# Attention and two feed-forward layers on one core: the second layer's matmul operands placed in either 64-byte half of a 128-byte stretch

## Chip, core and metric

One Trainium2 chip, one of its cores. The metric is the device time of one execution of the whole program, in microseconds; of several executions the median is given.

## What is computed

Three stages follow each other, all in fp32 accuracy. A Performer attention (random features, exponentials, a quotient) on q, k and v gives 2304 tokens of 512 features; two feed-forward layers act on these:

```python
def _moe_ref(x, w_a, w_b, w_out) -> np.ndarray:      # d_model 512, d_ff 1536
    a = x @ w_a
    b = x @ w_b
    return (a * b @ w_out).astype(np.float32)
...
def _moe2_ref(x, w_in, w_out) -> np.ndarray:         # d_model 512, d_ff 2048
    h = np.maximum(x @ w_in, 0.0)
    return (h * h @ w_out).astype(np.float32)
...
    x = np.ascontiguousarray(attn_out.transpose(0, 2, 1, 3)).reshape(B * S, H * D)
    x = _moe_ref(x=x, **moe_kwargs)
    return _moe2_ref(x=x, **moe2_kwargs)
```

Inputs are drawn in double precision; a weight arrives as two 32-bit words an element.

## The kernel before

**Split operands.** TensorE works on `float32r`. To keep fp32 accuracy each operand is held as a high part and a low part, and each product is three matmuls: high·high, high·low, low·high. `TERMS` (pairs of stationary part, moving part) is `((0, 0), (0, 1), (1, 0))`, so of three matmuls that follow each other the moving part goes high, low, high and the stationary part high, high, low. ScalarE and VectorE make the parts: `split` (L145 to L175) for weights, L728 and L729 for the tokens of the second layer, L784 to L787 for the hidden values.

**Stages.** Attention runs up to about 535 us, from 150 us on beside the first layer (phase A, `a_units`, matmuls of L610 and L635). The second layer (phase B, `b_units`) runs from about 650 us to the end. It is the part that the change touches.

**Phase B.** The 2304 tokens are cut into five blocks (`BB`): four of 512 and one of 256. For each block the loop over f goes through 16 slices of 128 hidden features. A slice takes 12 matmuls of L777 (four chunks kc of 128 input features, three terms each): stationary is a 128x128 piece of the weight `wi2[f]`, moving is the token tile `ys[i]`, 512 columns wide, 256 in the last block. ScalarE takes the sum out of PSUM with a Relu (L784), VectorE squares it (L785), ScalarE writes the high part (L786) and VectorE the low part (L787) into the tile `ss`. Then `outs(f - 1)` issues the matmuls of L764 of the slice before: for each 128 tokens of the block three matmuls, 12 in a wide block and 6 in the last. There stationary is a piece of `ss`, moving is `wo2[f]`, 512 columns in all blocks. So the stream of TensorE is 12 of L777, 12 (or 6) of L764, and so on; the hidden values of a slice are wanted one slice later.

**Where the tiles lie.** A weight pair (`wi2[f]` and `wo2[f]`) is one tile of `get_pair`, laid out `[pair, part, 512]`. Slice 0 has a pool of its own (`w2`), slices 1 to 12 reuse the 12 buffers of phase A's weights (`w`), slices 13 to 15 have a third pool (`w2r`). The token tile is `[chunk, part, columns]`, `ss` is `[part, columns]`. As the program is built, every `float32r` operand of phases A and B, moving or stationary, starts at a multiple of 128 bytes in its partition. In the attention there is another case: the tile `S`, stationary in the matmuls of L351 (moving is `OM`, 256 columns, at a multiple of 128), starts at byte 139,968 on the k side, which is 64 past a multiple of 128, and at byte 153,056 on the q side, which is 96 past one. The 128-column pieces of `S` lie 512 bytes apart, so they all keep that place.

**What sets the order.** One stream of instructions for each engine, in the order of the code; tiles in pools bring the waits. TensorE's weight load is an instruction of its own that runs beside the matmul ahead of it (engine PEld in the rows).

Of the kernel before, what the change touches and what calls it, by code (L numbers as in the profile page):

```python
# [9 lines left out]
F32R = mybir.dt.float32r  # L10
I32 = mybir.dt.int32
U32 = mybir.dt.uint32
U16 = mybir.dt.uint16
ACTF = mybir.ActivationFunctionType
ALU = mybir.AluOpType
# [20 lines left out]
def f32(ap):  # L36
    return ap.bitcast(F32)
# [7 lines left out]
def kernel(  # L45
# [17 lines left out]
    FA = w_out.shape[0] // 128  # L63
    FB = w_out2.shape[0] // 128
    KC = DM // 128
    NP = H // 2
    SM = 512
    ST = S - SM
# [73 lines left out]
    def split(raw, t):  # L142

        n = raw.shape[1]
        up = raw[:, :, :, 1]
        u = raw[:, :, :, 0]
        a = top["cut"].tile([128, 2, 512], F32, tag="a", name="a")[:, 0:n]
        p = top["cut"].tile([128, 2, 512], F32, tag="p", name="p")[:, 0:n]  # L150
        nc.scalar.activation(out=a, in_=f32(up), func=ACTF.Copy, scale=WORD_SCALE)  # L151
        nc.scalar.activation(  # L152
            out=u, in_=raw.bitcast(U16)[:, :, :, 1], func=ACTF.Copy, scale=2.0 ** 7,
        )
        nc.vector.tensor_scalar(
            out=i32(p), in0=i32(a), scalar1=3, scalar2=0x7FFFF000,
            op0=ALU.logical_shift_left, op1=ALU.bitwise_and,
        )
        nc.vector.scalar_tensor_tensor(  # L159
            out=i32(p), in0=i32(a), scalar=-0x80000000, in1=i32(p),  # L160
            op0=ALU.bitwise_and, op1=ALU.bitwise_or,
        )
        nc.scalar.copy(out=t[:, :, 0, :], in_=p)
        nc.vector.scalar_tensor_tensor(  # L164
            out=u.bitcast(U32), in0=up.bitcast(U32), scalar=23, in1=u.bitcast(U32),
            op0=ALU.logical_shift_left, op1=ALU.bitwise_or,
        )
        nc.vector.tensor_scalar(
            out=i32(a), in0=i32(p), scalar1=-0x00800000, scalar2=None,
            op0=ALU.bitwise_and,  # L170
        )
        nc.vector.scalar_tensor_tensor(
            out=t[:, :, 1, :], in0=u.bitcast(U32), scalar=2.0 ** -43, in1=a,
            op0=ALU.mult, op1=ALU.mult,
        )  # L175

# [26 lines left out]
        while any(x[1] == key for x in waiting):  # L203
            split_next()

    def get_pair(key, steps, pool, tag, *parts):
        t = pool.tile([128, 2, 2, 512], F32R, tag=tag, name=tag)
        load_split(key, parts, t, steps)
        return t[:, 0], t[:, 1]


    actx = ExitStack()
# [386 lines left out]
    def a_units():  # L599
# [4 lines left out]
        g_t, yp, part = {}, {}, {}  # L604

        def proj(ps, w, x):
            wv = w.rearrange("p a (k f) -> p a k f", k=KC)
            for kc in range(KC):
                for s_, m_ in TERMS:
                    nc.tensor.matmul(  # L610
                        ps, lhsT=wv[:, s_, kc, :], rhs=x[..., kc, m_, :],
                        start=(kc == 0 and (s_, m_) == TERMS[0]),
                        stop=(kc == KC - 1 and (s_, m_) == TERMS[-1]),
                    )
# [99 lines left out]

    wi2, wo2 = {}, {}

    BB = [(i * N, min(2, NBLK - i) * N) for i in range(0, NBLK, 2)]
    ys = {}
    op_pool = []

    def y_load(i, pool):
        w_ = BB[i][1]
        t = pool.tile([128, KC, 2, w_], F32R, tag="yx", name=f"yx{i}")
        ys[i] = t
        for c in range(KC):
            r = ypool.tile([128, w_], F32, tag="ys", name="yraw")
            nc.sync.dma_start(out=r, in_=y_d[i][:, c, :])
            nc.scalar.copy(out=t[:, c, 0, :], in_=r)  # L728
            nc.vector.tensor_tensor(  # L729
                out=t[:, c, 1, :], in0=r, in1=f32(t[:, c, 0, :]), op=ALU.subtract  # L730
            )

    def out_rows(c0):

# [17 lines left out]
    def b_units(i):  # L752


        y = ys[i]
        c0, w_ = BB[i]
        s_t, op = {}, {}

        def outs(f):
            for t in range(w_ // 128):  # L760
                if f == 0:
                    op[t] = bank(t, [128, DM], f"o{t}")
                for s_, m_ in TERMS:
                    nc.tensor.matmul(  # L764
                        op[t], lhsT=s_t[f][:, s_, t * 128:(t + 1) * 128], rhs=wo2[f][:, m_, :],
                        start=(f == 0 and (s_, m_) == TERMS[0]),
                        stop=(f == FB - 1 and (s_, m_) == TERMS[-1]),
                    )

        gp = wide_pool[0]  # L770
        for f in range(FB):
            need(("b", f))
            ps = bank(4 + f % 4, [128, w_], "ph")
            wv = wi2[f].rearrange("p a (k f) -> p a k f", k=KC)
            for kc in range(KC):
                for s_, m_ in TERMS:
                    nc.tensor.matmul(  # L777
                        ps, lhsT=wv[:, s_, kc, :], rhs=y[:, kc, m_, :],
                        start=(kc == 0 and (s_, m_) == TERMS[0]),
                        stop=(kc == KC - 1 and (s_, m_) == TERMS[-1]),  # L780
                    )
            r = gp.tile([128, w_], F32, tag="t", name="r")
            s_t[f] = gp.tile([128, 2, w_], F32R, tag="gs", name="ss")
            nc.scalar.activation(out=r, in_=ps, func=ACTF.Relu, scale=1.0 / W_SCALE)  # L784
            nc.vector.tensor_tensor(out=r, in0=r, in1=r, op=ALU.mult)  # L785
            nc.scalar.copy(out=s_t[f][:, 0, :], in_=r)  # L786
            nc.vector.tensor_tensor(  # L787
                out=s_t[f][:, 1, :], in0=r, in1=f32(s_t[f][:, 0, :]), op=ALU.subtract
            )
            if f:  # L790
                outs(f - 1)
            yield f
        outs(FB - 1)
        for t in range(w_ // 128):
            o = op_pool[0].tile([128, DM], F32, tag="o", name="o_s")
            nc.scalar.mul(out=o, in_=op[t], mul=1.0 / W_SCALE)
            for p0, cnt, r0, st in out_rows(c0 + 128 * t):
                nc.sync.dma_start(
                    out=out[r0:r0 + st * (cnt - 1) + 1:st, :], in_=o[p0:p0 + cnt, :]
                )  # L800
# [36 lines left out]
    def get_wo(n):  # L837
        if n >= len(wo_order):
            return
        pi, f = wo_order[n]  # L840
        if f in wo_made:
            need(("o", f))
            wo[pi, f] = wop.tile([128, 2, 512], F32R, tag="wo", name="wo")
            nc.sync.dma_start(out=f32(wo[pi, f]), in_=wo_d[f])
        else:
            wo_made.add(f)
            wo[pi, f] = wop.tile([128, 2, 512], F32R, tag="wo", name="wo")
            load_split(
                ("o", f), [(w_out, f, True)], wo[pi, f].unsqueeze(1), 3,
                lambda: nc.sync.dma_start(out=wo_d[f], in_=f32(wo[pi, f])),  # L850
            )

# [5 lines left out]
    def get_w2():  # L858
# [7 lines left out]
            po = (wpool, "w")  # L866
        else:
            po = (w2["r"], "w2r")
        wi2[f], wo2[f] = get_pair(("b", f), 1, *po, (w_in2, f, False), (w_out2, f, True))

    W_FIRST = 2

# [122 lines left out]
```

## Time and profile before

| | |
|---|---|
| median of three runs | 1052.57 us (1050.89 to 1053.95) |
| the profiled execution | 1052.61 us |
| its span, first to last instruction | 1050.8 us |
| TensorE matmul busy | 1024.0 us, 97% of the span |
| weight loads busy (beside the matmuls) | 873.6 us, 83% |
| VectorE, ScalarE busy | 526.8 us (50%), 471.2 us (45%) |
| granted TensorE clock, mean | 0.998 of 2.4 GHz |

A matmul's shown duration runs from its start to the arrival of its last result; since matmuls are pipelined, the next one starts long before. What a matmul costs is the distance from start to start. It is read from the chain of the work that ended last, or from the timeline, which merge equal matmuls: the time of a group of 12 divided by 12. The duration still tells something: it grows when a matmul is held up on its way.

### The profile page before, as it was taken

The page shows a single profiled execution, that of the slowest core. Times are in us where ns is not written, and L with a number is a line of the kernel's source. Part 1 is how long each engine was busy: PE and PEld are TensorE (multiplying, and loading weights), DVE is VectorE, ACT ScalarE, POOL GpSimd, SP SyncE. Part 2 cuts the span into 40 slices and gives each one's busy share as a digit, 9 for nine tenths or more (in the row PEclk, how much of TensorE's full clock was granted, in tenths as well). Part 3 has the DMA queues.
Part 4 walks back from the last instruction along what each step waited for, and adds up shares of the span by engine and source line. Part 5 has one row for each costly group of instructions (what it writes and reads, how often), then busy time and mean ns, then how long its engine had stood idle before and what let it go on. Part 6 is the DMA issues. An engine that isn't in the chain of part 4 may idle for free.

```text
span 1050.8 us, 14948 instructions
## 1 busy us (share of the span) xinstructions
PE 1024.0 (97%) x5641; PEld 873.6 (83%) x5641; DVE 526.8 (50%) x1274; ACT 471.2 (45%) x1079; POOL 28.9 (3%) x54
## 2 busy tenths in 40 slices
PE   4899999999999999999999999999999999999998
PEld 3789989999988877788888888788788888888887
DVE  4788885665654445444337987722222322322222
ACT  4887757554455443333326665522322322322232
POOL 3100101000000000000000000000000000000000
PEclk9999999999999999999999999999999999999999
DMA  6846864663432211312227664300200200100010
GB/s 166 242 148 205 267 233 120 210 209 95 142 105 80 63 46 56 95 62 70 66 87 264 230 220 174 107 1 0 81 1 1 71 1 1 51 1 1 0 41 21
DMA packets 83144, 105.90 MB, mean 101 GB/s; under 512 B 26240, under 2 KB 65152, under 8 KB 83072
## 3 DMA queue, kind: packets, MB, share of 16 engines
q1 hardware_dynamic: 81536, 103.37, 30.7%
q0 software_dynamic: 1536, 1.58, 0.5%
q8 instruction: 45, 0.74, 0.3%
q14 instruction: 27, 0.22, 0.1%
HBM read 87.62 MB, written 17.30 MB: 100 GB/s over the span
## 4 chain that ended last, share of the span: by engine, by line
PE 88%; DVE 4%; DMA 3%; ACT 3%; issue 1%; SPq 1%; ACTq 0%; DVEq 0%
PE abw L610 19%; PE o L764 19%; PE ph L777 18%; PE y L635 12%; PE ab L610 7%; PE ps_n L481 3%; PE ps_p L285 2%; PE ps_kv L423 2%; PE ps_p L351 2%; PE ps_qt L474 1%; DMA raw<-in_moe_w_out_dram 1%; PE ps_t L330 1%; DMA qn<-in_q_dram 1%; DVE p L159 1%; PE ps_x L492 1%
## 5 line engine op out<-in xcount | busy, mean ns | idle before, releaser
L635 PE MATMUL y<-gs,wo 128*128 128x256 f32 (+1 forms) x864 | 177.2, 345 | 0.0
L764 PE MATMUL o<-w,ss 128*128 128x512 f32 x702 | 170.9, 390 | 1.4 <-ACT ss L786 1.4
L777 PE MATMUL ph<-yx,w 128*128 128x512 f32 (+1 forms) x780 | 169.8, 368 | 0.0
L777 PEld LDWEIGHTS ph<-yx,w 128*128 128x128 f32 x780 | 137.4, 188 | 25.3
L785 DVE TENSOR_TENSOR r<-r 128x512 f32<-128x512 f32 (+1 forms) x80 | 51.1, 639 | 209.8 <-ACT r L784 209.8
L764 PEld LDWEIGHTS o<-w,ss 128*128 128x128 f32 x702 | 130.5, 188 | 29.7 <-ACT ss L786 2.2
L635 PEld LDWEIGHTS y<-gs,wo 128*128 128x128 f32 x864 | 136.6, 190 | 15.2
L610 PE MATMUL abw<-x_all,w 128*128 128x512 f32 x576 | 146.6, 398 | 0.0
L784 ACT ACTIVATE r<-ph 128x512 f32<-128x512 f32 (+1 forms) x80 | 44.5, 556 | 208.4 <-PE ph L777 208.2
L610 PE MATMUL ab<-x_all,w 128*128 128x256 f32 x864 | 132.9, 295 | 0.3 <-DVE x_all L549 0.2
L610 PEld LDWEIGHTS abw<-x_all,w 128*128 128x128 f32 x576 | 105.5, 189 | 19.2
L610 PEld LDWEIGHTS ab<-x_all,w 128*128 128x128 f32 x864 | 115.0, 193 | 1.5 <-DVE x_all L549 0.5
L787 DVE TENSOR_TENSOR ss<-r,ss 128x512 fp32r<-128x512 f32 (+1 forms) x80 | 51.1, 639 | 46.6 <-ACT ss L786 40.0
L610 PE MATMUL abw<-x_mid,w 128*128 128x512 f32 x288 | 73.1, 400 | 0.0
L786 ACT CAST ss<-r 128x512 fp32r<-128x512 f32 (+1 forms) x80 | 46.2, 577 | 51.5 <-DVE r L785 51.5
L610 PEld LDWEIGHTS abw<-x_mid,w 128*128 128x128 f32 x288 | 52.1, 189 | 9.8
L358 DVE CUSTOM_DVE_ANT_0 c<-ps_p,c 128x128 f32<-128x128 f32 x152 | 37.8, 287 | 32.5 <-ACT c L356 32.0
L701 ACT CAST gs<-a_s 128x256 fp32r<-128x256 f32 (+1 forms) x96 | 40.6, 433 | 28.3 <-DVE a_s L700 28.1
L164 DVE SCALAR_TENSOR_TENSOR raw<-raw 128x1024 uint32<-128x1024 uint32 (+1 forms) x40 | 42.5, 1062 | 13.4 <-ACT raw L152 13.3
L152 ACT ACTIVATE raw<-raw 128x1024 int32<-128x1024 uint16 (+1 forms) x40 | 40.8, 1020 | 11.4 <-DMA raw<-in_moe_w_out_dram 9.3
L702 DVE TENSOR_TENSOR gs<-a_s,gs 128x256 fp32r<-128x256 f32 (+1 forms) x96 | 42.8, 454 | 5.3 <-ACT gs L701 4.2
L151 ACT ACTIVATE a<-raw 128x1024 f32<-128x1024 f32 (+1 forms) x40 | 40.6, 1014 | 10.9 <-DMA raw<-in_moe_w_out_dram 5.6
(109 smaller groups left out, 1212.9 us busy)
## 6 DMA issues: line engine op xcount, KB each, us to landing
wo<-wo_d SPq DMA_DIRECT2D x60, 512.0 KB, 3.5
raw<-in_moe_w_out_dram SPq DMA_DIRECT2D x28, 512.0 KB, 4.8
raw<-in_moe_w_in_dram SPq DMA_DIRECT2D x16, 512.0 KB, 3.9
raw<-in_moe_w_a_dram SPq DMA_DIRECT2D x12, 512.0 KB, 4.8
raw<-in_moe_w_b_dram SPq DMA_DIRECT2D x12, 512.0 KB, 6.1
wo_d<-wo SPq DMA_DIRECT2D x12, 512.0 KB, 3.4
kn<-in_k_dram SPq DMA_DIRECT2D x16, 256.0 KB, 3.5
V<-in_v_dram SPq DMA_DIRECT2D x16, 256.0 KB, 3.4
```

Of the source, the lines that this page charges most:

```text
L151: nc.scalar.activation(out=a, in_=f32(up), func=ACTF.Copy, scale=WORD_SCALE)
L152: nc.scalar.activation(out=u, in_=raw.bitcast(U16)[:, :, :, 1], func=ACTF.Copy, scale=2.0 ** 7,)
L164: nc.vector.scalar_tensor_tensor(out=u.bitcast(U32), in0=up.bitcast(U32), scalar=23, in1=u.bitcast(U32), op0=ALU.logical_shift_left, op1=A ...
L610: nc.tensor.matmul(ps, lhsT=wv[:, s_, kc, :], rhs=x[..., kc, m_, :], start=(kc == 0 and (s_, m_) == TERMS[0]), stop=(kc == KC - 1 and (s_, ...
L635: nc.tensor.matmul(y_part(pi, f, c), lhsT=wo[pi, f][:, s_, c * 128:(c + 1) * 128], rhs=g[:, m_, :],  start=(f == f0 and (wide or c % 2 == ...
L702: nc.vector.tensor_tensor(out=g[:, 1, c], in0=a_s, in1=f32(g[:, 0, c]), op=ALU.subtract)
L764: nc.tensor.matmul(op[t], lhsT=s_t[f][:, s_, t * 128:(t + 1) * 128], rhs=wo2[f][:, m_, :], start=(f == 0 and (s_, m_) == TERMS[0]), stop=( ...
L777: nc.tensor.matmul(ps, lhsT=wv[:, s_, kc, :], rhs=y[:, kc, m_, :], start=(kc == 0 and (s_, m_) == TERMS[0]), stop=(kc == KC - 1 and (s_, m ...
L784: nc.scalar.activation(out=r, in_=ps, func=ACTF.Relu, scale=1.0 / W_SCALE)
L785: nc.vector.tensor_tensor(out=r, in0=r, in1=r, op=ALU.mult)
L786: nc.scalar.copy(out=s_t[f][:, 0, :], in_=r)
L787: nc.vector.tensor_tensor(out=s_t[f][:, 1, :], in0=r, in1=f32(s_t[f][:, 0, :]), op=ALU.subtract)
```

## The change

Only the places of phase B's operands change; the number, the kind, the order and the waits of all instructions are as before on every engine, row for row.

- `get_pair` makes the tile of a weight pair 1024 words for each of its two halves as before, or, with `odd` given, 1056 words. A word is four bytes, and `LINE` is 16 words, 64 bytes. With `odd=(a, b)` the high part starts `64*a` bytes after a multiple of 128, the low part `64*b` bytes. This is used for the slices 13 (1, 1), 14 (0, 1) and 15 (1, 0). It holds for both weights of a pair, the stationary one of L777 and the moving one of L764.
- `y_load` puts 64-byte gaps between the eight pieces of a token tile so that the piece of chunk c and part m starts at `64 * (Y_ODD[i % 4](c, m) mod 2)` past a multiple of 128: c + m in blocks 0 and 4, m in block 1, c in block 2, 0 in block 3.
- `ss` gets a gap too: `S_ODD` gives the places of its high and low part, (0, 0) in blocks 0 and 4, (0, 1) in block 1, (1, 1) in block 2, (1, 0) in block 3.
- `split` and `load_split` get the two parts as two views. Of phase A's operands none moves. The token tiles grow by 512 bytes a partition, `ss` by 128, the three last weight buffers by 256; the pools around them move by multiples of 128 bytes.

Below, a place is called odd when it is 64 bytes past a multiple of 128, else even. Counted over the built program of the changed kernel, in phase B:

| block | columns of L777 | L777 matmuls followed by a matmul whose moving operand has the other place | the same for L764 | place of `ss`, high and low |
|---|---|---|---|---|
| 0 | 512 | 190 of 192 | 20 of 192 | even, even |
| 1 | 512 | 129 of 192 | 19 of 192 | even, odd |
| 2 | 512 | 63 of 192 | 19 of 192 | odd, odd |
| 3 | 512 | 1 of 192 | 19 of 192 | odd, even |
| 4 | 256 | 191 of 192 | 10 of 95 | even, even |

So 470 matmuls with 512 columns and 191 with 256 are followed by a moving operand of the other place. The stationary operand that is loaded beside a matmul has the other place than this matmul's moving operand for 659 matmuls with 512 columns and 98 with 256. Before, all these counts are zero.

```diff
+    LINE = 16
+    SPAN = 1024 + 2 * LINE
...
-        nc.scalar.copy(out=t[:, :, 0, :], in_=p)
+        nc.scalar.copy(out=t[0], in_=p)
...
-            out=t[:, :, 1, :], in0=u.bitcast(U32), scalar=2.0 ** -43, in1=a,
+            out=t[1], in0=u.bitcast(U32), scalar=2.0 ** -43, in1=a,
...
-    def get_pair(key, steps, pool, tag, *parts):
-        t = pool.tile([128, 2, 2, 512], F32R, tag=tag, name=tag)
-        load_split(key, parts, t, steps)
-        return t[:, 0], t[:, 1]
+    def get_pair(key, steps, pool, tag, *parts, odd=None):
+        t = pool.tile([128, 2, SPAN if odd else 1024], F32R, tag=tag, name=tag)
+        at = (LINE * odd[0], 512 + LINE * (2 - odd[1])) if odd else (0, 512)
+        hi, lo = (t[:, :, o:o + 512] for o in at)
+        load_split(key, parts, (hi, lo), steps)
+        return [(hi[:, x], lo[:, x]) for x in range(2)]
...
+    Y_ODD = [lambda c, m: c + m, lambda c, m: m, lambda c, m: c, lambda c, m: 0]
+    S_ODD = [(0, 0), (0, 1), (1, 1), (1, 0)]
+    W_ODD = {13: (1, 1), 14: (0, 1), 15: (1, 0)}
...
-        t = pool.tile([128, KC, 2, w_], F32R, tag="yx", name=f"yx{i}")
-        ys[i] = t
+        t = pool.tile([128, KC * 2 * w_ + 2 * KC * LINE], F32R, tag="yx", name=f"yx{i}")
+        ys[i] = {}
+        for c in range(KC):
+            for m in range(2):
+                o = (2 * c + m) * (w_ + LINE) + LINE * ((2 * c + m + Y_ODD[i % 4](c, m)) % 2)
+                ys[i][c, m] = t[:, o:o + w_]
...
-                        op[t], lhsT=s_t[f][:, s_, t * 128:(t + 1) * 128], rhs=wo2[f][:, m_, :],
+                        op[t], lhsT=s_t[f][s_][:, t * 128:(t + 1) * 128], rhs=wo2[f][m_],
...
-                        ps, lhsT=wv[:, s_, kc, :], rhs=y[:, kc, m_, :],
+                        ps, lhsT=wi2[f][s_][:, kc * 128:kc * 128 + 128], rhs=y[kc, m_],
...
-            s_t[f] = gp.tile([128, 2, w_], F32R, tag="gs", name="ss")
+            st = gp.tile([128, SPAN], F32R, tag="gs", name="ss")
+            s_t[f] = tuple(
+                st[:, o:o + w_]
+                for o in (LINE * S_ODD[i % 4][0], 512 + LINE * (2 - S_ODD[i % 4][1]))
+            )
...
-        wi2[f], wo2[f] = get_pair(("b", f), 1, *po, (w_in2, f, False), (w_out2, f, True))
+        wi2[f], wo2[f] = get_pair(("b", f), 1, *po, (w_in2, f, False), (w_out2, f, True), odd=W_ODD.get(f))
```

## Rows read from the trace of the kernel before

**Rows 1.** The page: engines, the granted clock, the chain by engine and line.

```profile
PE 1024.0 (97%) x5641; PEld 873.6 (83%) x5641; DVE 526.8 (50%) x1274; ACT 471.2 (45%) x1079; POOL 28.9 (3%) x54
...
PEclk9999999999999999999999999999999999999999
...
PE 88%; DVE 4%; DMA 3%; ACT 3%; issue 1%; SPq 1%; ACTq 0%; DVEq 0%
PE abw L610 19%; PE o L764 19%; PE ph L777 18%; PE y L635 12%; PE ab L610 7%; PE ps_n L481 3%; PE ps_p L285 2%; PE ps_kv L423 2%; PE ps_p L351 2%; PE ps_qt L474 1%; DMA raw<-in_moe_w_out_dram 1%; PE ps_t L330 1%; DMA qn<-in_q_dram 1%; DVE p L159 1%; PE ps_x L492 1%
```

**Rows 2.** Busy time by stretch of phase B, in us, with counts and granted clock.

```profile
661.00:750.00 89.00, 88.52 (x389) 72.44 (x388) 34.43 (x49) 29.63 (x48) 0.00 (x0) 1.00 0.13 42
750.00:825.00 75.00, 75.00 (x332) 61.91 (x331) 20.53 (x30) 17.98 (x30) 0.00 (x0) 1.00 0.00 1
835.00:910.00 75.00, 75.00 (x333) 62.10 (x332) 18.65 (x28) 16.76 (x29) 0.00 (x0) 1.00 0.00 0
914.00:998.00 84.00, 84.00 (x372) 69.54 (x372) 21.93 (x32) 20.97 (x35) 0.00 (x0) 1.00 0.03 13
```

**Rows 3.** Chain in order of time: start, us, engine and line; a wide block.

```profile
805.20 2.72 PE o L764 x12
```

**Rows 4.** Timeline of TensorE, wide block: start, us, instructions; moving operand from both pools.

```profile
802.32 2.88 PE L777 MATMUL ph<-yx,w 128*128 128x512 f32 x12
805.04 2.88 PE L764 MATMUL o<-w,ss 128*128 128x512 f32 x12
807.76 2.88 PE L777 MATMUL ph<-yx,w2r 128*128 128x512 f32 x12
810.48 2.88 PE L764 MATMUL o<-w,ss 128*128 128x512 f32 x12
```

**Rows 5.** Timeline of TensorE in the last block.

```profile
1007.24 1.55 PE L764 MATMUL o<-w,ss 128*128 128x512 f32 x6
1008.63 1.60 PE L777 MATMUL ph<-yx,w 128*128 128x256 f32 x12
1010.06 1.55 PE L764 MATMUL o<-w,ss 128*128 128x512 f32 x6
```

**Rows 6.** Durations in ns, min/median/max: line 764 in 750 to 820 us.

```profile
L764 PE MATMUL o<-w,ss x144: 389/389/389, 750.6 to 813.0; 128*128 128x512 f32 x144
```

**Rows 7.** The same, lines 764 and 777 in the last block, 1007 to 1043 us.

```profile
L764 PE MATMUL o<-w,ss x72: 389/394/398, 1007.2 to 1039.4; 128*128 128x512 f32 x72
...
L777 PE MATMUL ph<-yx,w x124: 277/283/283, 1006.8 to 1035.3; 128*128 128x256 f32 x124
```

**Rows 8.** One matmul of line 777 beside which no weights are loaded.

```profile
L777 PE MATMUL ph<-yx,w 128*128 128x512 f32 x1 | 0.4, 388 | 0.0
```

**Rows 9.** One matmul at 316.7 us: line L610, an odd piece of S loaded beside.

```profile
L610 PE MATMUL abw<-x_all,w 128*128 128x512 f32 x1 | 0.4, 388 | 0.0
```

**Rows 10.** One matmul at 437.1 us: line L610, a piece 96 bytes past loaded beside.

```profile
L610 PE MATMUL abw<-x_mid,w 128*128 128x512 f32 x1 | 0.4, 391 | 0.0
```

**Rows 11.** Timeline of TensorE at a stop: the first slices of phase B.

```profile
658.38 3.02 PE L764 MATMUL o<-w,ss 128*128 128x512 f32 x12 [0.93 <-ACT ss L786]
661.24 1.07 PE L777 MATMUL ph<-yx,w 128*128 128x512 f32 x4
```

**Rows 12.** The page's groups of the engines that write `ss` and the token tiles.

```profile
L785 DVE TENSOR_TENSOR r<-r 128x512 f32<-128x512 f32 (+1 forms) x80 | 51.1, 639 | 209.8 <-ACT r L784 209.8
L784 ACT ACTIVATE r<-ph 128x512 f32<-128x512 f32 (+1 forms) x80 | 44.5, 556 | 208.4 <-PE ph L777 208.2
L787 DVE TENSOR_TENSOR ss<-r,ss 128x512 fp32r<-128x512 f32 (+1 forms) x80 | 51.1, 639 | 46.6 <-ACT ss L786 40.0
L786 ACT CAST ss<-r 128x512 fp32r<-128x512 f32 (+1 forms) x80 | 46.2, 577 | 51.5 <-DVE r L785 51.5
```

More of the change, by code (lines that the diff above doesn't have):

```diff
@@ L606, in proj @@
         def proj(ps, w, x):
-            wv = w.rearrange("p a (k f) -> p a k f", k=KC)
             for kc in range(KC):
@@ L610, in proj @@
                     nc.tensor.matmul(
-                        ps, lhsT=wv[:, s_, kc, :], rhs=x[..., kc, m_, :],
+                        ps, lhsT=w[s_][:, kc * 128:kc * 128 + 128], rhs=x[..., kc, m_, :],
                         start=(kc == 0 and (s_, m_) == TERMS[0]),
@@ L727, in y_load @@
             nc.sync.dma_start(out=r, in_=y_d[i][:, c, :])
[L728 to L731, printed above, removed]
+            hi, lo = ys[i][c, 0], ys[i][c, 1]
+            nc.scalar.copy(out=hi, in_=r)
+            nc.vector.tensor_tensor(out=lo, in0=r, in1=f32(hi), op=ALU.subtract)
     def out_rows(c0):
@@ L773, in b_units @@
             ps = bank(4 + f % 4, [128, w_], "ph")
-            wv = wi2[f].rearrange("p a (k f) -> p a k f", k=KC)
             for kc in range(KC):
@@ L782, in b_units @@
             r = gp.tile([128, w_], F32, tag="t", name="r")
-            s_t[f] = gp.tile([128, 2, w_], F32R, tag="gs", name="ss")
+            st = gp.tile([128, SPAN], F32R, tag="gs", name="ss")
[3 more added lines that the diff above has]
+            )
             nc.scalar.activation(out=r, in_=ps, func=ACTF.Relu, scale=1.0 / W_SCALE)
             nc.vector.tensor_tensor(out=r, in0=r, in1=r, op=ALU.mult)
-            nc.scalar.copy(out=s_t[f][:, 0, :], in_=r)
+            nc.scalar.copy(out=s_t[f][0], in_=r)
             nc.vector.tensor_tensor(
-                out=s_t[f][:, 1, :], in0=r, in1=f32(s_t[f][:, 0, :]), op=ALU.subtract
+                out=s_t[f][1], in0=r, in1=f32(s_t[f][0]), op=ALU.subtract
             )
@@ L848, in get_wo @@
             load_split(
-                ("o", f), [(w_out, f, True)], wo[pi, f].unsqueeze(1), 3,
+                ("o", f), [(w_out, f, True)],
+                tuple(wo[pi, f][:, m].unsqueeze(1) for m in range(2)), 3,
                 lambda: nc.sync.dma_start(out=wo_d[f], in_=f32(wo[pi, f])),
```

## The prediction

> **What bounds the kernel now.** I read the page first: TensorE is busy for 97% of the span, it carries 88% of the chain that ended last, and its granted clock is at the upper level, 2.4 GHz, in every slice [rows 1]. So I went to phase B alone, the only place where operands move. There TensorE is busy without a gap in whole stretches, while VectorE and ScalarE are busy for about a quarter of them (20.53 and 17.98 of 75 us) [rows 2]. The reader is to see that only the distance from one matmul to the next counts here.
>
> That distance comes from the chain: 12 matmuls take 2.72 us, so 226.7 ns each [rows 3]. The same time stands between the starts of the groups in the timeline, for L777 and L764, and whether the weights came from the pool `w` or from `w2r` [rows 4]. 512 columns at the granted 2.4 GHz take 213.3 ns if one column goes in a cycle; that rate is an estimate which the last block bears out, since 256 columns less cost 226.7 - 119.2 = 107.5 ns. So 13.3 ns lie over the columns in each matmul. All matmuls of such a stretch are alike to the nanosecond: duration 389 at least, in the middle and at most [rows 6]. The last block is another case: 12 matmuls of 256 columns take 1.43 us (119.2 ns each) and 6 of 512 take 1.39 us (231.7 ns each) [rows 5], with durations up to 398 and 283 instead of 389 and 277 [rows 7]. [...] After a stop the same is seen for a few matmuls: 12 take 661.24 - 658.38 = 2.86 us, 0.14 more than in step, of which a first unhidden weight load is a part [rows 11]. So there are two states: in step, 226.7 ns, and out of step, some 5 ns more.
>
> As a sum, a wide block is 16 slices of 24 matmuls, 16 x 5.44 = 87.0 us; four are 348.2 us. The last is 16 x (1.43 + 1.39) = 45.1 us. These 393 us are all that the change can act on.
>
> **What the change does to it, part by part.**
>
> *Instructions.* None is added, removed or moved, on any engine, and the waits are the same ones. Cost 0.
>
> *The writers of the parts.* ScalarE and VectorE write equal shapes at other places. For a wide slice the four steps take 0.556 + 0.639 + 0.577 + 0.639 = 2.41 us [rows 12], against 5.44 us of matmuls, and the result is wanted a whole slice later. If odd places doubled them (no row says so) they would still be hidden in the wide blocks. Cost 0. The cover is thinner in the last block, 2.82 us a slice, but there `ss` is even as before, and so are its writers.
>
> *Odd weights beside an even matmul, or the reverse.* 659 matmuls of 512 columns get this. The trace has the case already: pieces of S in the attention are odd and are loaded beside matmuls of phase A with even moving operands. Where the stream is in step or about to be, there are four of these (at 316.7, 333.7, 361.5 and 372.1 us); all four last 388 ns, one stands as the example [rows 9]. In step with an even weight load it is 389 [rows 6], and with no weight load beside it 388 [rows 8]. So an odd load costs the matmul nothing, and an even one a single nanosecond. The price is between -1 and 0 ns, since 388 is also the time without a load. Sum: 659 x 1 = 0.7 us gained at most. I take half, -0.3 us, because the next matmul need not start earlier when the end comes earlier. For the 98 of 256 columns the rows give no direct price; 277 and 283 [rows 7] bound it at 6 ns either way, 0.6 us, and I take 0.
>
> The reverse (odd moving, even weights) I take to be the same, because shifting both by 64 bytes should be like shifting neither: the pools `w` and `w2r` start at other multiples of 128, and no place but the lowest seven bits of the address differs from what the rows already cover.
>
> Does the place matter at all? A piece of S that starts 96 past a multiple of 128 gives 391 [rows 10], three more than the odd one. [...]
>
> *A moving operand that follows one of the other place.* This is the part without a row: before, all moving operands of `float32r` are even. It concerns 470 matmuls of 512 columns and 191 of 256. Below, the gain cannot be more than the 13.3 ns over the columns: 470 x 13.3 = 6.3 us, and for 256 columns, down to 106.7, 191 x 12.5 = 2.4 us, together 8.6 us. Above, the nearest row is a matmul held up out of step, 398 - 389 = 9 ns at the worst [rows 7]: 661 x 9 = 5.9 us. I take 0, by the row that is nearest: pieces that start in different buffers, pools and distances from a multiple of 1024 follow each other within [rows 4] and change nothing.
>
> *Places of the buffers.* They move by multiples of 128 bytes and bring no new wait. Cost 0.
>
> The sum is -0.3 us: 1052.61 - 0.3 = 1052.3 for the profiled execution (1050.8 of it span, 1.8 around it). Its 1052.61 is within 0.1 us of the median 1052.57, so the forecast is **1052.3**.
>
> **The rivals.**
>
> *Faster: the next stream starts sooner.* If the 13.3 ns come from the start of each moving stream having to wait for the half in which the last one began, a change of place saves half of it, the 6.7 ns of 16 columns (64 bytes): 661 x 6.7 = 4.4 us, **1048.2**. For it: 13.3 ns are just the time of 32 columns, two such halves. Against: the time is the same wherever the buffers start, and out of step no group is faster than in step [rows 3, 5]. It passes 0.3% (3.2 us, about what a measurement of this kernel tells from no change) from 4.8 ns a change of place.
>
> [...]
>
> *Slower: the step is lost.* In step, all pairs of matmul and load have the same relation of places. The change mixes them from matmul to matmul: in L777 of blocks 0, 1 and 2 (576 matmuls) and in L764 of blocks 1 and 3 (384). If an odd load lets its matmul go 1 ns earlier and the next even one then meets a bad moment, the stream stays out of step, at 231.7 instead of 226.7 ns [rows 3, 5]: 960 x 5.0 = 4.8 us, **1057.4**. For it: each stop shows how easily the state is left [rows 11], and in the last block it is left in each slice. Against: the stream falls back into step within a dozen matmuls by itself. It decides from 3.3 ns a matmul.
>
> [...]
>
> *Slower: neighbours collide.* Two streams that meet in the same half, the end of one and the start of the next, cost 16 columns: 661 x 6.7 = 4.4 us, **1057.0**. For it: nothing in the rows; against it the same.
>
> **How the numbers follow.** No change beyond noise, as forecast: 0.58, with its own range 1050.4 to 1054.2 (the three runs' spread and the bounds of ±0.6 us). The next stream sooner: 0.19. Step lost: 0.15. Collision: 0.08. Of the forecast's cases nearly all stay within 0.3%, and of each rival a part comes out too small to be told: faster by over 0.3% 0.19, within 0.3% 0.60, slower by over 0.3% 0.21. The range reaches just past both rivals' times on the near side: 1048.0 to 1057.5; about half of each side's rivals lie beyond, some 0.2 in all.
>
> **What would show it.** In the profile of the changed kernel the groups of 12 in the chain should stay at 2.72 us in blocks 0 to 3, with durations of 388 and 389. Groups at 2.64 in L777 of block 0 but 2.72 in block 3 would speak for the first rival; durations of 393 to 398 in the mixed blocks and 2.78 a group, for the second; 2.80 in L777 of block 0 alone, with L764 untouched, for the third. The prediction is wrong if a change of place has a price of 5 ns or more either way.

## The result and the profile after

The changed kernel takes 1059.97 us (median of three runs, 1059.48 to 1060.34), against 1052.57 before: a ratio of 1.0071, 95% interval 1.0046 to 1.0095. It is slower by 7.4 us, and lies 2.5 us above the end of the forecast range. The profiled execution took 1059.48 us, its span 1057.7.

The lines of the changed kernel's page that answer [rows 1] and [rows 12]. Its line 773 is line 764 of before, 785 is 777, and 796 to 799 are 784 to 787; the columns are busy us, mean ns of one, idle time before and its releaser.

```profile
PE 1030.4 (97%) x5641; PEld 872.5 (82%) x5641; DVE 526.9 (50%) x1274; ACT 470.9 (45%) x1079; POOL 29.6 (3%) x54
...
PEclk9999999999999999999999999999999999999999
...
L773 PE MATMUL o<-w,ss 128*128 128x512 f32 x702 | 174.0, 395 | 0.7 <-ACT ss L798 0.7
L785 PE MATMUL ph<-yx,w 128*128 128x512 f32 (+1 forms) x780 | 172.6, 371 | 0.0
...
L797 DVE TENSOR_TENSOR r<-r 128x512 f32<-128x512 f32 (+1 forms) x80 | 51.1, 638 | 217.2 <-ACT r L796 217.2
...
L796 ACT ACTIVATE r<-ph 128x512 f32<-128x512 f32 (+1 forms) x80 | 44.4, 555 | 215.5 <-PE ph L785 215.5
...
L799 DVE TENSOR_TENSOR ss<-r,ss 128x512 fp32r<-128x512 f32 (+1 forms) x80 | 51.1, 639 | 46.7 <-ACT ss L798 40.5
...
L798 ACT CAST ss<-r 128x512 fp32r<-128x512 f32 (+1 forms) x80 | 46.2, 578 | 51.4 <-DVE r L797 51.4
```

The counts of instructions are those of before, the clock is granted in full (mean 1.000, before 0.998), and the four steps of VectorE and ScalarE last what they lasted (555, 638, 578 and 639 ns). In these rows only TensorE's matmuls of phase B are longer. Busy time by stretch, the stretches of [rows 2]:

```profile
661.00:750.00 89.00, 88.57 (x381) 70.94 (x380) 34.57 (x49) 29.65 (x48) 0.00 (x0) 1.00 0.14 44
750.00:825.00 75.00, 75.00 (x325) 60.75 (x324) 18.01 (x26) 15.86 (x26) 0.00 (x0) 1.00 0.00 0
835.00:910.00 75.00, 75.00 (x326) 60.72 (x325) 19.39 (x29) 17.05 (x28) 0.00 (x0) 1.00 0.03 9
914.00:998.00 84.00, 84.00 (x366) 68.33 (x365) 22.29 (x34) 22.43 (x39) 0.00 (x0) 1.00 0.05 16
```

TensorE is busy for all of the time, as before, but gets fewer matmuls done: 381, 325, 326 and 366 where [rows 2] have 389, 332, 333 and 372. The loss is spread over all four wide blocks. The chain in order of time (start, us, engine and line) shows its size, against the 2.72 of [rows 3]:

```profile
786.34 2.76 PE o L773 x12
789.10 2.79 PE ph L785 x12
791.89 2.81 PE o L773 x12
794.70 2.78 PE ph L785 x12
```

And the durations in ns (min/median/max) of line 773 in 750 to 820 us, where [rows 6] had 389/389/389:

```profile
L773 PE MATMUL o<-w,ss x145: 387/394/402, 749.7 to 816.5; 128*128 128x512 f32 x145
L773 PEld LDWEIGHTS o<-w,ss x144: 187/188/192, 752.5 to 816.3; 128*128 128x128 f32 x144
```

From the starts of all matmuls: the first products of blocks 0 to 3 now follow each other every 231.5 ns (before 226.7), the second ones every 231.8 (before 226.9). That is 768 x 4.8 + 768 x 4.9 = 7.4 us. In the last block the 192 of 256 columns gain 1.1 ns each and the 96 of 512 lose 1.2, which cancels to 0.1 us. So the difference lies in the matmuls whose operands were moved, and the question is what about their places costs it. (The profiled spans differ by 6.9 us: in the changed kernel the stops in phase B are 1.0 us shorter, and it starts 0.6 us later.)

Against what the description of the change says, a few operands of phase A move too. The last phase A pass takes its gate tiles `gs` from the same buffers as `ss`, so these now alternate by 128 bytes. By the addresses of the built program, 72 of the wide matmuls of L638 between 571 and 651 us have a moving operand 128 bytes off their weights; they start every 232.7 ns, the others of that stretch every 226.9. That is 0.4 us.

A word on places. In the kernel before, the moving and the stationary operand of every `float32r` matmul of phases A and B start at 128 past a multiple of 256 bytes. In the changed kernel they start at 0, 64, 128 or 192 past one: the gaps of 64 bytes between pieces add up, so that pieces meant to be even lie 128 bytes apart (in a token tile, `(2c+m) * 64` bytes more or less), and the `ss` buffers, 4224 bytes long, alternate by 128. "Alike" means below: the same place within 256 bytes.

### The profile page after: what moved, and what is told of

Its sections match the earlier page's. It is cut to its first block, busy times and chain, and to the rows that moved or that the text cites. A ratio compares the mean times of both kernels' runs of the same rounds, so it can differ in the third digit from the quotient of the medians.

```text
span 1057.7 us, 14948 instructions
## 1 busy us (share of the span) xinstructions
PE 1030.4 (97%) x5641; PEld 872.5 (82%) x5641; DVE 526.9 (50%) x1274; ACT 470.9 (45%) x1079; POOL 29.6 (3%) x54
## 3 DMA queue, kind: packets, MB, share of 16 engines
q0 software_dynamic: 1536, 1.58, 0.5%
## 4 chain that ended last, share of the span: by engine, by line
PE 86%; DMA 5%; DVE 4%; ACT 3%; issue 1%; SPq 1%; ACTq 0%; DVEq 0%
PE o L773 19%; PE abw L613 19%; PE ph L785 18%; PE y L638 12%; PE ab L613 6%; PE ps_n L485 2%; PE ps_p L355 2%; DMA raw<-in_moe_w_b_dram 2%; PE ps_kv L427 2%; PE ps_p L289 2%; PE ps_qt L478 1%; DMA raw<-in_moe_w_out_dram 1%; PE ps_t L334 1%; DVE p L161 1%; ACT a L153 1%
## 5 line engine op out<-in xcount | busy, mean ns | idle before, releaser
L638 PE MATMUL y<-gs,wo 128*128 128x256 f32 (+1 forms) x864 | 177.6, 345 | 0.0
L773 PE MATMUL o<-w,ss 128*128 128x512 f32 x702 | 174.0, 395 | 0.7 <-ACT ss L798 0.7
L785 PE MATMUL ph<-yx,w 128*128 128x512 f32 (+1 forms) x780 | 172.6, 371 | 0.0
L638 PEld LDWEIGHTS y<-gs,wo 128*128 128x128 f32 x864 | 136.6, 190 | 15.5
```

The source lines that it names most:

```text
L638: nc.tensor.matmul(y_part(pi, f, c), lhsT=wo[pi, f][:, s_, c * 128:(c + 1) * 128], rhs=g[:, m_, :],  start=(f == f0 and (wide or c % 2 == ...
L773: nc.tensor.matmul(op[t], lhsT=s_t[f][s_][:, t * 128:(t + 1) * 128], rhs=wo2[f][m_], start=(f == 0 and (s_, m_) == TERMS[0]), stop=(f == F ...
L785: nc.tensor.matmul(ps, lhsT=wi2[f][s_][:, kc * 128:kc * 128 + 128], rhs=y[kc, m_], start=(kc == 0 and (s_, m_) == TERMS[0]), stop=(kc == K ...
```

## The experiments

Three questions: which property of the places counts (the mixing, the distance, one operand's own place); how much each part of the change costs; and whether places can be used to gain.

**1. The changed kernel's combinations with one distance.** These three keep its combination table and gather the pieces of one place, so that two operands differ by exactly one distance or not at all. Against the changed kernel:

```diff
-            for m in range(2):
-                o = (2 * c + m) * (w_ + LINE) + LINE * ((2 * c + m + Y_ODD[i % 4](c, m)) % 2)
+        odd = {(c, m): Y_ODD[i % 4](c, m) % 2 for c in range(KC) for m in range(2)}
+        for n, (c, m) in enumerate(sorted(odd, key=lambda x: (odd[x], x))):
+            o = n * w_ + STEP * odd[c, m]
```

`STEP` is 16, 32 or 64 words; `ss` and the weight pairs are padded by 256 bytes likewise.

> The changed kernel's combination of places, block by block, but each part lies whole at 0 or at 64 bytes past a multiple of 256 plus 128 (all pieces of one place together, then those of the other), so that operands differ by 64 bytes alone. In the changed kernel they also differ by 128. Theory A (a difference of 64 bytes alone takes the stream out of step): matmuls of 512 columns at 230 to 232 ns, some 1060 us. Theory B (it takes a difference of 128 bytes): 226.7 ns, 1052 to 1053 us. Theory C (not the places but the gaps, the buffers' bases or the writers): as the changed kernel, 1060 us, here and in the next two.

> The same combination with 128 bytes in place of 64, so that all operands lie at a multiple of 128 but differ within 256. Theory A: in step, 226.7 ns, 1052 to 1053 us. Theory B: 230 to 232 ns, some 1060 us. Theory C: 1060 us.

> The same combination with 256 bytes in place of 64: all operands again alike within 256 bytes, as in the kernel before, with the gaps and grown buffers still there. Theories A and B: in step, 226.7 ns, 1052 to 1053 us. Theory C: 1060 us. A fourth reading, that any difference of place does it, also gives 1060 us.

With 64 bytes: 1059.0 us, ratio 1.0064 (1.0043 to 1.0084), as slow as the changed kernel. With 128 bytes: 1057.22, 1.0048 (1.0032 to 1.0065). With 256 bytes: 1052.14, 1.0001 (0.9989 to 1.0014), nothing lost. So theory C, which hung on the gaps, falls; of theories A and B, each of which wanted one distance alone, neither holds, since both distances cost. The gaps, the order of the pieces and the mixing of addresses as such cost nothing in this run; what counts in these three is the place within 256 bytes. Timelines of TensorE (start, us, instructions), first the 256-byte kernel in block 1, then the 128-byte kernel in block 0:

```profile
806.25 2.88 PE L773 MATMUL o<-w,ss 128*128 128x512 f32 x12
808.97 2.88 PE L785 MATMUL ph<-yx,w2r 128*128 128x512 f32 x12
811.68 2.88 PE L773 MATMUL o<-w,ss 128*128 128x512 f32 x12
```

```profile
689.76 2.88 PE L773 MATMUL o<-w,ss 128*128 128x512 f32 x12
692.48 2.92 PE L785 MATMUL ph<-yx,w 128*128 128x512 f32 x12
695.24 2.88 PE L773 MATMUL o<-w,ss 128*128 128x512 f32 x12
```

In the first, groups start 2.72 us apart. In the second, line 773 (all alike in block 0) takes 692.48 - 689.76 = 2.72, and line 785, half of whose moving pieces are 128 bytes off, 695.24 - 692.48 = 2.76. The starts within such groups of 12, read from the trace, show which matmul pays (ns from one start to the next; "even" and "odd" here for the two places of the kernel named):

```
128 bytes, block 0, ph (moving even, odd, ...; weights even)      226 235 225 235 225 235 225 235 225 235 225 235
128 bytes, block 1, ph (moving even, odd, even; weights even)     227 234 226 226 234 226 227 234 226 227 234 226
128 bytes, block 1, o  (moving even; weights even, even, odd)     226 233 234 227 232 234 227 232 235 226 233 234
64 bytes,  block 0, o  (all alike, after a mixed ph)              230 230 236 229 232 231 227 226 227 227 226 227
```

Row 2: only the matmul with the odd moving operand pays; the next one, whose moving operand changes place again, does not. Row 3: the second matmul of three is alike with its own weights, and pays while the odd weights for the third are loaded; the third pays for its own weights. So with 128 bytes a wide matmul keeps its step if its moving operand is alike with the weights in use and with those being loaded: over blocks 0 to 3 of this kernel the 701 such matmuls take 227.6 ns on average, the 822 others 232.6. Row 4: with 64 bytes, once all are alike again, the stream needs six matmuls (229 to 236 ns) to get back to 226 and 227. There the loss can't be booked matmul by matmul: in the 64-byte kernel the 701 alike matmuls take 230.7 ns, the others 232.4. A size for the loss, as an estimate from the kernel before: 256 columns more take 226.7 - 119.9 = 106.8 ns there, so 16 columns (64 bytes of a row) take 6.67 ns, about what the dearest of the means below lose (233.0 to 233.6 ns against 226.7 and 226.9). That the loss comes in steps of this size is not shown: in the 128-byte kernel single distances go from 224 to 241 ns.

**2. One shift for all, no mixing.** All token and `ss` tiles of phase B start 64, 128, 192 or 32 bytes higher than before, the weights stay; the last one moves everything by 64 bytes, weights included. The first diff is that of the kernels with one shift, against the changed kernel; the second is the whole edit of the last one, against the kernel before.

```diff
+    Y_ODD = [lambda c, m: 1] * 4
+    S_ODD = [(1, 1)] * 4
+    W_ODD = {}
```

```diff
+    shift = ctx.enter_context(tc.tile_pool(name="shift", bufs=1))
+    shift.tile([128, 16], F32, name="shift")
...
-    edge.tile([128, 24], F32, name="edge")
+    edge.tile([128, 72], F32, name="edge")
```

> No mixing: in all blocks every token piece and every part of ss lies 64 bytes further than in the kernel before, the weights stay. So moving and loaded operand always differ by 64 bytes within a group of 12, and neighbours of a group are alike. If it is the change of place from matmul to matmul that takes the stream out of step: in step, 226 to 227 ns, 1052 to 1053 us, and with 388 ns durations perhaps 0.7 us less. If the difference between a moving operand and the weights loaded beside it does it: 230 to 232 ns in all groups, 1060 us.

> As the kernel with all tokens and ss 64 bytes further, but 128: the moving operand of L777 is 128 past the loaded weights, in L764 the loaded ss is 128 past the moving one. Theory A: out of step in all groups, 229 to 234 ns, some 1058 us. If 128 is less bad than 64, as the combination with 128 hinted (1057.2 against 1059.0): 228 to 231 ns, 1055 to 1057 us.

> The same with 192 bytes. Against the kernel with 64, the two relations change sides: L777 has now a moving operand 64 bytes ahead of the loaded weights in place of behind, L764 the reverse. If only the relation counts, L777 takes what L764 took there (233.3 ns) and L764 what L777 took (231.5 ns), 1060 us in all; if the side (moving or loaded) or the line counts, the numbers stay with the lines.

> Token and relu-squared tiles of blocks 0 to 4 all start 32 bytes higher than in the kernel before, weights stay: the shift is half of a 64-byte place, so it tells whether what counts is the 64-byte place within 256 bytes or any difference of the addresses. Theory A (the place counts in whole lines of 64 bytes, and an operand that starts in the middle of a line counts as one of the line's): in step, 226.7 ns, 1052.3 us. Theory B (any difference counts, since a 2048-byte row that starts in the middle of a line touches one line more): out of step as at 64, 128 and 192 bytes, 231 to 233 ns, 1058 to 1060 us. Rival (a smaller difference than 64 bytes is a smaller loss): half, 229 ns, 1055.5 us.

> The kernel before with every tile of the program, on both sides of the memory, 64 bytes further: all moving and all loaded operands of both layers are odd. Theory A (what counts is the difference, within 256 bytes, between a matmul's moving operand and the weights loaded beside it): in step, 226.7 ns, as before, 1052 us. Rival (what counts is the place itself, against something that stands still): both layers out of step, 12 x 1824 wide-block matmuls aside also those of phase A, 1060 us or more.

| shift of tokens and `ss` | time, us | ratio (95%) | ph, blocks 0-3, ns | o, blocks 0-3, ns | ph of 256 columns, ns |
|---|---|---|---|---|---|
| none (before) | 1052.57 | 1 | 226.7 | 226.9 | 119.9 |
| 32 bytes | 1060.98 | 1.0081 (1.0059 to 1.0104) | 233.1 | 233.6 | 117.4 |
| 64 bytes | 1060.22 | 1.0072 (1.0056 to 1.0088) | 231.1 | 233.3 | 118.2 |
| 128 bytes | 1059.80 | 1.0078 (1.0061 to 1.0095) | 233.0 | 233.0 | 120.2 |
| 192 bytes | 1058.35 | 1.0067 (1.0044 to 1.0090) | 233.3 | 231.3 | 116.2 |
| 64 bytes, weights too | 1052.50 | 1.0002 (0.9989 to 1.0014) | 226.7 | 226.9 | 120.0 |

The last three columns are means from start to start. Timelines of TensorE in block 1, first with 128 bytes, then with 32, then with all operands moved by 64:

```profile
807.14 2.96 PE L773 MATMUL o<-w,ss 128*128 128x512 f32 x12
809.94 2.96 PE L785 MATMUL ph<-yx,w2r 128*128 128x512 f32 x12
812.74 2.96 PE L773 MATMUL o<-w,ss 128*128 128x512 f32 x12
```

```profile
805.41 2.96 PE L785 MATMUL ph<-yx,w 128*128 128x512 f32 x12
808.21 2.96 PE L773 MATMUL o<-w,ss 128*128 128x512 f32 x12
```

```profile
805.66 2.88 PE L766 MATMUL o<-w,ss 128*128 128x512 f32 x12
808.38 2.88 PE L779 MATMUL ph<-yx,w2r 128*128 128x512 f32 x12
811.10 2.88 PE L766 MATMUL o<-w,ss 128*128 128x512 f32 x12
```

2.80 us a group in the first two, against 2.72 in the last. Three things follow. The mixing is not needed for the loss: a difference that is the same everywhere costs 7 to 8.5 us by the ratios. The place 64 bytes up is not bad in itself: with the weights moved along, nothing is lost (1052.50 us, 226.7 and 226.9 ns). And the relation has a sign: with 64 bytes the first products pay 4.4 ns and the second ones 6.4, with 192 bytes it is the other way round (6.6 and 4.4), as the tokens are the moving operand in the first product and `ss` the stationary one in the second. The 32 bytes answer a last question on the size: half of a 64-byte stretch already costs as much as the whole (233.1 and 233.6 ns). The means hide a pattern: with 128 bytes the first products of block 1 go at 229 and 238 ns by turns.

**3. Weights in use, or weights being loaded?** All high parts of weights, tokens and `ss` get one place and all low parts another, 64 bytes off. Then each moving piece lies like the weights that are loaded beside it, always, and like those in use in one matmul of three.

```diff
-    wpool = ctx.enter_context(tc.tile_pool(name="wpool", bufs=FA))
+    wpool = two("wp", FA, ctx)
...
+    Y_ODD = [lambda c, m: m] * 4
+    S_ODD = [(0, 1)] * 4
```

(`two` opens two pools, one for high and one for low parts, with gaps of 64 and 192 bytes.)

> All high parts of phase B even, all low parts odd, moving and stationary ones, weights included. Moving places then go even, odd, even, so that two of three matmuls are followed by one of the other place, but each matmul's moving operand always has the place of the weights that are loaded beside it (those of the next matmul). Theory A (the difference to the weights loaded beside): wide blocks in step, 226.7 ns, groups of 12 at 2.72 us. Rival 1 (the change of moving place from matmul to matmul): out of step, 230 to 234 ns. Rival 2 (the difference to the weights in use): out of step. Phase A has weights with odd low parts beside even tokens here, so it may be up to 10 us slower and the total says nothing; phase B alone is read.

The one run took 1060.84 us; its phase A is disturbed too, since the weight pools serve both phases, so only its phase B is read here. Timeline of TensorE, first wide block:

```profile
700.15 2.94 PE L794 MATMUL ph<-yx,w 128*128 128x512 f32 x12
702.92 2.94 PE L782 MATMUL o<-w,ss 128*128 128x512 f32 x12
705.70 2.94 PE L794 MATMUL ph<-yx,w 128*128 128x512 f32 x12
```

2.77 and 2.78 us a group: 231.1 to 231.2 ns a matmul in blocks 0 and 1, 232.1 to 232.2 in blocks 2 and 3. To lie like the weights being loaded is not enough here. That the weights in use count as well doesn't follow from this run alone, because its moving operand also changes place from matmul to matmul; row 3 above shows it at 128 bytes, where the moving operand never moves and the third matmul, alike with the weights being loaded, pays for its own.

The mean of blocks 0 and 1 fits the estimate of 6.67 ns as a price for two matmuls of three: 226.7 + 2/3 x 6.67 = 231.1. By the same count the changed kernel, in which 386 of the 1632 matmuls of 512 columns in phase B are alike with both (from the addresses of its operands), should stand at 226.7 + 0.76 x 6.67 = 231.8; it stands at 231.5 and 231.8. But this is an agreement of means. In blocks 0 and 1 of this kernel the matmuls alike with both take 232 to 233 ns and one of the two other kinds 229 to 230; blocks 2 and 3 lie 1 ns above the count; and in blocks 0 to 3 of the changed kernel the 363 alike with both take 230.9 ns, the others 231.9.

**4. The change part by part.** The first kernel has the changed kernel's token tiles alone, the second its `ss` tiles alone; the diff is that of the first. The third part, the weights of slices 13 to 15, was not run alone.

```diff
-    W_ODD = {13: (1, 1), 14: (0, 1), 15: (1, 0)}
+    W_ODD = {}
...
-            st = gp.tile([128, SPAN], F32R, tag="gs", name="ss")
+            st = gp.tile([128, 2, w_], F32R, tag="gs", name="ss")
```

> Only the token tiles of phase B are laid out as in the changed kernel (64-byte gaps, another combination for each block); relu-squared tiles and the last three weight pairs lie as before. Theory (a wide matmul keeps its 226.7 ns only if its moving operand lies alike, within 256 bytes, with the weights in use and with those being loaded): the first products of blocks 0, 1 and 2 lose their step (576 matmuls, 231 to 232 ns, 2.9 us), the second products are alike everywhere but begin out of step after them and fall back in within about half of a group of 12 (mean 229 ns in these three blocks, 1.5 us), block 3 stays at 226.7: about 4.4 us, 1055 to 1057.5 us against 1052.3. Rival (the cost belongs to the stationary operand alone): 1052.3 us, 226.7 ns everywhere. Rival (the whole cost belongs to the moving operand): 1059.9 us.

> Only the relu-squared tiles are laid out as in the changed kernel; token tiles and weight pairs lie as before. Theory (alike with the weights in use and those being loaded): the second products of blocks 1, 2 and 3 lose their step (576 matmuls, 231 to 234 ns, 3 to 4 us), the first products between them are alike and fall back in within some six matmuls (mean 228 to 229 ns, 1 to 1.5 us), block 0 stays at 226.7: about 4 to 5.5 us, 1056 to 1058 us against 1052.3. Rival (the cost belongs to the moving operand alone): 1052.3 us. Rival (the whole cost belongs to the stationary operand): 1059.9 us.

Tokens alone: 1055.91 us, ratio 1.0039 (1.0026 to 1.0053). `ss` alone: 1056.96, 1.0049 (1.0030 to 1.0068). Both times were as expected, but both expectations missed one block, so the agreement is in part luck: the tokens of block 3 and the `ss` of block 0, even by the table, lost their step too (230.0 and 232.6 ns instead of 226.7), because even pieces lie 128 bytes apart in this layout, which the expectation had forgotten. By the distances in blocks 0 to 3 the parts cost 5.4 and 4.2 us, together 9.6, against 7.4 in the changed kernel; the times alone can't tell (4.1 and 5.2 us by the ratios, give or take 1.4 and 2.0). The sum is larger because alone, each part leaves the other product alike, and that one pays too while it gets back into step: 1.9 us of the 5.4 and 0.7 of the 4.2. Timelines of the tokens-alone kernel, block 1 and block 3:

```profile
805.84 2.93 PE L773 MATMUL o<-w,ss 128*128 128x512 f32 x12
808.61 2.95 PE L785 MATMUL ph<-yx,w2r 128*128 128x512 f32 x12
...
935.92 2.92 PE L785 MATMUL ph<-yx,w 128*128 128x512 f32 x12
938.68 2.88 PE L773 MATMUL o<-w,ss 128*128 128x512 f32 x12
941.40 0.85 PE L785 MATMUL ph<-yx,w 128*128 128x512 f32 x3
```

In block 1 the first product differs by 64, 128 and 192 bytes, and the second, all alike, still takes 2.77 us; ten of its twelve matmuls go by before it is back at 227 ns. In block 3, after a first product of 2.76 whose pieces differ by 128 bytes alone, it takes 941.40 - 938.68 = 2.72 and is in step at once, as in block 0 of the 128-byte kernel.

**5. A version to beat both.** In the table above the matmuls of 256 columns do the opposite: with tokens 192 bytes up (64 below the weights within 256 bytes) they start every 116.2 ns instead of 119.9. Phase A has 1296 of that size. So this kernel leaves every wide operand of phase A and of blocks 0 to 3 alike and puts the narrow moving ones 64 bytes below the weights.

```diff
-    x_all = xpool.tile([128, 3, KC, 2, N], F32R, name="x_all")
+    x_all = xpool.tile([128, 3 * XW + 16], F32R, name="x_all")
...
-        return top["x"] if i == 5 else x_all[:, 0:2]
+        return top["x"] if i == 5 else x_view(XW + 16, 2)
```

> A kernel with the kernel before's order, in which only the moving operands of the 256-column matmuls are moved: the narrow token tiles and gate tiles of phase A and block 4's token tile lie 64 bytes below the weights within 256, every 512-column matmul of phase A and of blocks 0 to 3 lies alike as before (block 4's 96 second products get stationary tiles at the other place). Theory, from u192, whose 256-column matmuls started every 115.8 ns instead of 119.3: what is lost by a difference at 512 columns is gained at 256. 192 in block 4 and up to 1296 in phase A x 3.5 ns give 0.7 to 5 us, the upper end if phase A's narrow matmuls are paced as block 4's are (most of them start every 118 to 120 ns in the kernel before too): 1047.5 to 1051.5 us. Rival (in phase A the narrow matmuls are paced by the work between them, not by this step): 1051.3 to 1052.5, no difference that can be measured. Rival (any difference costs, and u192's 256-column matmuls were quick for another reason): above 1053.

1052.76 us, ratio 1.0000 (0.9988 to 1.0012): no gain, where 1047.5 to 1051.5 was expected. The groups of TensorE in phase A's narrow passes, 15 to 294 us (busy us, mean ns of one, idle before), first of the kernel before, then of this one:

```profile
L610 PE MATMUL ab<-x_all,w 128*128 128x256 f32 x864 | 132.9, 295 | 0.3 <-DVE x_all L549 0.2
L635 PE MATMUL y<-gs,wo 128*128 128x256 f32 x420 | 65.2, 293 | 0.0
```

```profile
L616 PE MATMUL ab<-x_all,w 128*128 128x256 f32 x864 | 129.9, 292 | 0.5 <-DVE x_all L555 0.4
L641 PE MATMUL y<-gs,wo 128*128 128x256 f32 x418 | 64.2, 291 | 0.0
```

The matmuls did become shorter, by 3 and 2 ns, and their means from start to start (distances under 260 ns, within one line) fell from 127.6 to 124.5 ns and from 127.3 to 124.8. But the first wide matmul starts at 293.77 us before and at 294.61 now, within the 291.7 to 294.7 of the other kernels, whose narrow passes are those of before. What lies over 260 ns in the distances behind the narrow matmuls grew from 4.8 to 7.0 us: in these two profiled executions the time came back as waiting. This speaks for the rival, that the work between the narrow matmuls paces them; one execution of each kernel, in a phase whose length differs by 3 us from one execution to the next, does not prove it. The 192 narrow matmuls of block 4 (116.3 ns) save 0.7 us, too little to be told.

## Why the prediction was wrong, step by step

*What bounds the kernel.* Right: phase B is bounded by the distance from one matmul to the next (TensorE is busy for 75.00 of 75.00 us in the stretches above), and 226.7 ns and some 5 ns more are what the result shows. The 213.3 ns for 512 columns stay an estimate: no run shows a clock in GHz, only the granted share (0.998 and 1.000). But with operands alike 256 columns more take 106.8 ns in the kernel before and 106.7 with all operands moved by 64 bytes, 2.40 columns a ns, which gives 213.4 to 213.6. Instructions and writers at no cost were right as well (the counts, and 555, 638, 578 and 639 ns above).

*"No place but the lowest seven bits of the address differs from what the rows already cover."* This is the step that failed first. In the kernel before, all these operands lie at 128 past a multiple of 256, so but for the single loads of `S` the rows covered one relation only, equality within 256 bytes. A shift of 128 bytes, which by this sentence is none, costs 6.3 ns a matmul on the first product and 6.1 on the second. For the same reason *places of the buffers, moves by multiples of 128 bytes, cost 0* was wrong: such moves put even pieces out of step, as the part-by-part runs showed, and cost the 0.4 us of phase A's gate tiles.

*Odd weights beside an even matmul, -1 to 0 ns.* This is the term of the sum that was mis-sized: four single loads were taken for the price in a stream. The duration was not what misled. In the four cases of [rows 9] the distance to the next start is 226 ns too, so it also said "free":

```profile
316.74 0.39 PE L610 MATMUL abw<-x_all,w 128*128 128x512 f32 x1
316.96 0.41 PE L351 MATMUL ps_p<-OM,S 128*128 128x256 f32 x2
```

And in the changed kernel the median duration of line 773 does rise, from 389 to 394, about as much as the distance. But each of the four is one wide matmul at the end of an alike stream, with narrow ones behind it. In the stream of the 128-byte kernel an alike matmul beside an odd load takes 232 to 233 ns from start to start instead of 226.7, and its neighbour with the odd weights 234. There the term should have been about +6 ns, not -0.5. At 64 bytes no run has the case pure: the loss spreads over the matmuls that follow. Why the four single loads cost nothing stays open: they differ from the stream in the distance (64 bytes), in being single and in what follows them.

*The reverse, odd moving beside even weights, taken as the same.* At 128 bytes nearly right as to sameness (234 to 235 ns against 232 to 233) and wrong in value. At 64 bytes the sign counts: 231.1 ns with the moving operand 64 above the weights, 233.3 with it 64 below. The reason that was given, that shifting both by 64 bytes is like shifting neither, held (1052.50 us).

*A moving operand that follows one of the other place, 0 ns.* Right at 128 bytes: after an odd moving operand the even one goes at 225 to 227. At 64 bytes it wasn't isolated. The rivals *the next stream starts sooner* and *neighbours collide* fall all the same, since both hang on a change of place from one stream to the next: the first products of block 3 of the changed kernel have 1 such change and go at 230.3 ns, and a shift without any change inside the groups of 12 costs 7 to 8.5 us.

*The rival "the step is lost".* This is what happened. Its price, 5.0 ns a matmul, is within 0.2 of the 4.8 and 4.9 measured, and its group time, 2.78, is in the chain. That the price fits is partly luck: it was read from the last block, where all operands are alike and narrow matmuls stand between the wide ones, and no run shows that the two losses have one cause. It was undersized in its count, 960 matmuls where 1536 lost the step, and so gave 1057.4. The count rested on mixing; but an offset that never changes costs as much, and the layout mixes within 256 bytes also in the groups that the table calls even. The argument against it, that the stream falls back by itself, holds only for groups that are alike, and there it took six matmuls of twelve (64-byte kernel, block 0) and ten (tokens alone, block 1). And it stood as a rival, not as the forecast, because the single cases of [rows 9] were taken for the price.

Whether a load takes anything from the running matmul has thus two answers in these runs. The single odd loads of the kernel before take nothing that shows (226 ns). In the 128-byte kernel a matmul that is alike with its own weights takes 232 to 233 ns when the weights loaded beside it lie 128 bytes off, and 226 to 227 when they do not.

What stays open is why. That operands which start at the same place within 256 bytes get on best (226.7 ns against 231.1 to 233.6), and that 256 columns go faster with some differences (116.2 to 118.2 ns against 119.9), is measured; what in the chip reads in which order was not seen in any run.

## What to carry to other kernels

Where a stage is an unbroken stream of wide `float32r` matmuls with a weight load each, as here, keep the moving operand and the weights at the same place within 256 bytes, and check the addresses after any padding: here a difference of 32 to 192 bytes cost 2 to 3% of each matmul and 0.7 to 0.8% of the kernel. Price such a change by the distance from start to start in a stream that has the change throughout; a single matmul, by its duration or by its distance, said that it was free. And before saying that the rows cover a case, list what is constant in all of them: a property that never varies in the trace has no price in it.

## What the chip showed that was not expected

- The stream of wide `float32r` matmuls went at 226.7 to 226.9 ns where its moving operands started at the same place within 256 bytes as its weights, and at 231.1 to 233.6 where all of them lay 32, 64, 128 or 192 bytes off; 256 bytes did nothing (2.72 us a group of 12, 1052.14 us). With 128 bytes a matmul paid both for the weights in use (234 to 235 ns) and for those being loaded (232 to 233).
- The matmuls of 256 columns in the last block went the other way: 119.9 ns alike, 116.2 with the moving operand 64 bytes below the weights, 117.4 and 118.2 with it 32 and 64 above, 120.2 at 128. It did not make the kernel faster (1052.76 us).
- When the operands were alike again, the stream was back in step at once after differences of 128 bytes (2.72 us for the next group of 12), and after six and ten matmuls in the two groups read where 64 bytes were among the differences.
